# One written order for all steps of a windowed-attention and feed-forward kernel

## The chip, the core and the metric

The kernel runs on one core of a Trainium2 chip. The metric is the device time of one execution in microseconds (us); below it is the median of three runs. The engines are TensorE (PE in the rows; its weight loads PEld), VectorE (DVE), ScalarE (ACT), GpSimd (POOL) and SyncE (SP); ACTq and SPq are the instructions with which ScalarE and SyncE start transfers.

## What is computed

The reference, cut to its core (batch 8, 8 heads, 576 positions, head size 64; window 64; 4608 tokens of width 512; hidden width 2048):

```python
scores = scale * np.matmul(q, k.transpose(0, 1, 3, 2))
scores = np.where((rel >= 0) & (rel < window), scores, -1e9)
attn = np.exp(scores - scores.max(axis=-1, keepdims=True))
attn = attn / (attn.sum(axis=-1, keepdims=True) + 1e-09)
x = np.matmul(attn, v)                      # heads side by side: 4608 x 512
h = x @ w_in
out = np.maximum(0.01 * h, h) @ w_out
```

## The kernel before

**Work and stages.** The tokens form nine chunks of 512. Chunks 0 to 2 go through the two large products directly: `early_first` (tile h, line 1143) makes 128 hidden rows of one chunk in 12 matmuls, in two halves of 6; `leak` (line 1157), `high_of` (1160, ScalarE) and `low_of` (1163, VectorE) turn them into a high and a low part, and `early_second` (tile acc, line 1152) multiplies those with `w_out` in four groups of 3 matmuls, two turns later. The first half of chunk 0 and part of chunk 1 have the same work under other names (lines 679 and 715). Chunks 3 to 8 go in three pairs, each by seven products in place of eight: `product` (tile m, line 1344) for the first matrix, `seventh` (tile z, line 1410) for the second. Every operand is a high and a low float32r part, so a product is three matmuls.

**Attention** runs in 36 blocks of 128 tokens, between these matmuls. For block m: `mask_to` (ScalarE, line 876) writes the mask into two banks, `scores_of` (TensorE, 64 small matmuls, line 525) adds the scores, `copy_of` (ScalarE, 890) copies them out, `max_of` (GpSimd, 899) takes the maximum over partitions, `minus_of` (VectorE, 906) subtracts it, `exp_of` (ScalarE, 910), `add_of` (GpSimd, 902) sums, `values_of` (TensorE, 32 small matmuls, line 958) multiplies with v. `values_of` writes into one of the two banks that the h tiles use in turn, so it must wait until `low_of` of the last turn in that bank has read it. A stay of TensorE with one or more of these small steps between two large ones is called a visit here.

**Weights.** Until about 130 us, VectorE and ScalarE make float32 weights out of float64 words (`bits` 472, `sign` 476, `size` 480, `clamp` 484, `join` 489, `split` 492 with a store to `w_single`, `rest` 498). Then `prepare` makes sums of weights for the seven products: `whole_of` (VectorE, 1257) or a fetch (1253), four `join_of` (VectorE, 1260), `high` (ScalarE, 1263), `prep_low` (VectorE, 1266), and two stores `keep` issued by ScalarE (1270, 1273). `x_build` reads rows of x back (line 1091), makes sums of them by four `sub` (VectorE, 1098), and splits them by ScalarE (1117) and `x_low` (VectorE, 1120); the first `product` needs all of it.

**What sets the order.** Each engine runs its instructions in the order in which the program issues them. The first part (536 steps in the numbering below, to about 128 us) was issued from the hand-written string `ORDER`, before anything else. All later steps are entries of a list `plan`, made by `op`, each with its engine, a cost and the steps it comes after; `arranged` sorted them: `forward` runs the plan through a model of the engines, the transfers and a rule for GpSimd against VectorE (`port_rule`), `latest` gives each step a due time, and some rounds of both, 14 of them nudged at random, end in the order. Transfers issued by ScalarE and SyncE take turns through eight semaphores (`LANES = 8` in the model), so an issue waits until the eighth transfer before it has landed, and whatever stands behind it on the issuing engine waits too.

Of the kernel before, what the change touches and what calls it, by code (L numbers as in the profile page):

```python
# [26 lines left out]
P = 128  # L27
# [31 lines left out]
q0 X6 S0 k1 raw0 q1 E0 P0 E1 bits0 sign0 raw1 v0 q2 k2 P1 X3 Z0 Z1 S1 abs0 E2 N0 exp0 X1 N1 bits1 sign1 abs1 clamp0  # L59
join0 clamp1 V0 sm0 join1 exp1 V1 E3 S2 chi0 raw2 chi1 raw3 rec0 sm1 rec1 bits2 sign2 y1 y0 P2 P3 N2 raw4 E4 rest1  # L60
rest0 E5 exp2 N3 exp3 T0 v1 V2 V3 k3 q3 abs2 H0 S3 v2 v3 q4 k4 sm2 P4 sub4 P5 rec2 sm3 L0 y2 rec3 clamp2 y3 exp4 V4 E6
T1 join2 H1 sub5 sm4 bits3 rec4 L1 exp5 X4 V5 P6 raw5 chi2 sign3 abs3 E7 bits4 rest2 sub6 sm5 clamp3 rec5 y4 y5 sign4
P7 M0 lk0 exp6 gh0 M1 abs4 gl0 T2 W0 join3 sub7 bits5 clamp4 V6 lk1 H2 exp7 raw6 L2 gh1 join4 V7 S4 chi4 raw7 chi3 gl1
sm6 sign5 sm7 rest4 rec7 rec6 rest3 M2 E8 abs5 y7 y6 T3 bits6 sign6 W1 lk2 H3 L3 clamp5 P8 M3 gh2 gl2 join5 v4 k5 q5
E9 S5 v5 q6 k6 raw8 lk3 gh3 chi5 abs6 sub8 bits7 exp8 gl3 M4 lk4 rest5 sign7 clamp6 W2 V8 P9 abs7 sub9 join6 gh4 raw9
M5 bits8 gl4 E10 sm8 sign8 exp9 chi6 W3 P10 clamp7 rec8 y8 join7 rest6 lk5 abs8 clamp8 gh5 V9 M6 W4 gl5 join8 bits9
sub10 sm9 sign9 rec9 y9 raw10 E11 raw11 chi7 P11 chi8 lk6 exp10 T4 gh6 abs9 rest8 rest7 bits10 M7 V10 W5 gl6 sign10
clamp9 H4 abs10 sub11 join9 L4 bits11 sm10 rec10 clamp10 y10 join10 lk7 raw12 exp11 gh7 gl7 S6 V11 chi9 rest9 sign11
W6 chi10 raw13 abs11 E13 E12 P12 rest10 sm11 bits12 clamp11 join11 rec11 y11 chi11 raw14 sign12 abs12 bits13 sign13
clamp12 sub12 join12 M8 T5 v6 q7 v7 k7 W7 lk8 gh8 H5 exp12 abs13 chi12 raw15 gl8 P13 bits14 L5 V12 sign14 clamp13  # L70
rest11 sub13 sm12 join13 rest12 rec12 S7 y12 E14 raw16 abs14 exp13 clamp14 join14 bits15 P14 W8 V13 M9 sub14 sm13
sign15 chi14 E15 exp14 chi13 abs15 lk9 gh9 P15 rec13 y13 V14 T6 rest14 rest13 sub15 M10 sm14 clamp15 gl9 rec14 join15
y14 exp15 raw17 H6 chi15 V15 W9 bits16 sign16 L6 lk10 gh10 abs16 raw18 sm15 rec15 gl10 y15 T7 H7 rest15 W10 clamp16
bits17 join16 sign17 L7 abs17 clamp17 join17 bits18 raw19 chi16 ev0 chi17 ev1 raw20 rest16 sign18 abs18 rest17 M11
bits19 clamp18 M12 lk11 gh11 gl11 lk12 gh12 sign19 join18 M13 W11 M14 gl12 abs19 raw21 chi18 lk13 bits20 clamp19
join19 chi19 raw22 sign20 rest18 rest19 W12 M15 gh13 gl13 abs20 W13 bits21 clamp20 sign21 join20 bits22 abs21 lk14
sign22 clamp21 join21 raw23 chi20 M16 gh14 gl14 W14 rest20 raw24 abs22 clamp22 join22 chi21 raw25 bits23 rest21 sign23
bits24 lk15 chi22 gh15 gl15 sign24 abs23 abs24 clamp23 join23 bits25 chi23 raw26 lk16 M17 W15 clamp24 sign25 rest22
join24 M18 abs25 gh16 raw27 clamp25 gl16 rest23 join25 W16 chi24 rest24 bits26 sign26 lk17 chi25 rest25 raw28 abs26
gh17 bits27 clamp26 gl17 sign27 join26 abs27 clamp27 join27 chi26 lk18 chi27 gh18 bits28 sign28 rest26 gl18 k8 q8 v8  # L80
W17 q9
|
abs28 raw29 clamp28 join28 bits29 raw30 sign29 rest27 abs29 bits30 chi28 clamp29 sign30 rest28 abs30 join29 clamp30
raw31 chi29 bits31 sign31 rest29 abs31 join30 clamp31 chi30 join31 rest30 chi31 rest31
"""
FEW = 5
# [19 lines left out]
SLACK, AHEAD, ROUNDS = 0.0, 10.0, 4  # L106
NUDGES = (
    652231581, 285970256, 32845751, 566537775, 247891063, 817061414, 899342503, 908597559, 243672113, 194115331,
    115674943, 420121951, 340751465, 165549087,
)  # L110
LAGS = 1.0
ENTER, LEAVE, SIGNAL, SLOW = 0.12, 0.2, 0.07, 0.6
BOTH_SBUF = {
    "wide_low": 1.22, "combine": 1.22, "whole_of": 0.69, "prep_low": 1.22, "sub": 0.38, "join_of": 0.41, "x_low": None,
    "low_early": 0.68, "join": 0.69, "sign": 0.69, "rest": 0.69,
}
COSTS = {
    ("DVE", "inverse_of"): 0.19, ("DVE", "whole_inverse_of"): 3.35, ("DVE", "bits"): 0.42, ("DVE", "clamp"): 0.42,
    ("ACT", "guard_of"): 0.2, ("ACT", "wide_high"): 1.05, ("ACT", "high"): 1.05, ("ACT", "exp_of"): 0.63, ("ACT", "leaky"): 0.63,
    ("ACT", "high_early"): 0.63, ("ACT", "whole_guard_of"): 0.63, ("ACT", "split"): 0.63, ("ACT", "size"): 0.68,  # L120
    ("POOL", "max_of"): 1.87, ("POOL", "add_of"): 3.3, ("POOL", "fill"): 0.76, ("PE", "scores_of"): 0.97, ("PE", "values_of"): 0.97,
}
RATE, EACH, LANDING = 460.0, 100.0, 3.9
SIZES = dict(fill=1024, load_qk=512, load_v=512, fetch=512, fetch_w=512, keep=512, spread_of=128, rows_of=4, compact_of=2)
LONGER = dict(compact_of=0.5, spread_of=0.6, load_v=0.5, send=-2.7, reload_of=-1.5, fetch_w=-1.5, store=-1.2)


def measure(plan):
    for x in plan:
        f = x["fn"]  # L130
        name = x["name"] = getattr(f, "func", f).__name__
        e = x["engine"]
        x["both"] = e == "DVE" and (name in BOTH_SBUF or x["us"] > 1.0 and name in ("minus_of", "product_of"))
        x["reduce"] = name in ("max_of", "add_of")
        x["visit"] = name in ("scores_of", "values_of")
        x["dma"] = bool(x["land"])
        x["lane"] = x["dma"] and e != "POOL"
        if x["both"]:
            x["us"] = BOTH_SBUF.get(name, 0.67) or x["us"]
        elif (e, name) in COSTS:  # L140
            x["us"] = COSTS[e, name]
        elif e == "ACT" and x["land"]:
            x["us"] = 0.5
        elif e == "ACT" and x["us"] < 0.7 and name != "<lambda>":
            x["us"] = 0.59
        elif e == "DVE" and x["us"] < 1.0:
            x["us"] = 0.69
        x["bytes"] = EACH + x.get("size", SIZES.get(name, 256.0))
        x["more"] = LANDING + LONGER.get(name, 0.0)
        x["users"] = []  # L150
    for x in plan:
        for a in x["after"]:
            a["users"].append(x)


def gap(a, x, slack):
    if a["engine"] == x["engine"] and not a["dma"]:
        return 0.0
    return max(SIGNAL, x["lag"] * LAGS) + (slack if a["dma"] else 0.0)


def visiting(x, before):
    return x["us"] + (ENTER if x["visit"] and not before else LEAVE if before and not x["visit"] else 0.0)


def port_rule(x, t, port, held):
    end = t + x["us"]
    if x["both"]:
        held = end = (port[1] if port[0] <= t < port[1] else t) + x["us"]
    if x["reduce"]:  # L170
        end = max(t, held) + x["us"]
        port = end - x["us"], end - (0.9 if x["name"] == "max_of" else 1.12)
    return end, port, held


class Transfers:
    def __init__(self, rate=RATE):
        self.rate, self.queues, self.now, self.left = rate, {}, 0.0, {}

    def busy(self):  # L180
        return [q for q in self.queues.values() if q]

    def next(self):
        qs = self.busy()
        return min((self.now + self.left[q[0]["n"]] * len(qs) / self.rate for q in qs), default=None)

    def advance(self, t):
        qs = self.busy()
        for q in qs:
            self.left[q[0]["n"]] -= (t - self.now) * self.rate / len(qs)  # L190
        self.now = t

    def landed(self, t):
        self.advance(t)
        return [q.pop(0) for q in self.busy() if self.left[q[0]["n"]] <= 1e-6]

    def add(self, x):
        self.queues.setdefault(x["engine"], []).append(x)
        self.left[x["n"]] = x["bytes"]


def forward(plan, key, slack, due=None):
    free = dict.fromkeys(("PE", "DVE", "ACT", "POOL", "SP"), 0.0)
    waiting = {e: [] for e in free}
    missing = {x["n"]: len(x["after"]) for x in plan}
    for x in plan:
        if not x["after"]:
            waiting[x["engine"]].append((0.0, x))
# [3 lines left out]
    moving = Transfers()  # L212

    def begins(y):
        ready, x = y
        if x["lane"] and len(lanes) >= LANES:
            return max(ready, done.get(lanes[-LANES]["n"], math.inf))
        a = cleared(x)
# [20 lines left out]
    while True:  # L239
# [14 lines left out]
        if best is None:  # L254
            break
# [1427 lines left out]
```

## Time and profile before

| what | us |
|---|---|
| median of three runs | 842.6 (841.9 to 842.64) |
| the profiled execution, whole time | 840.71 |
| its span, first to last instruction | 838.9 |
| TensorE busy in it | 828.8 |

The time of an execution is its span and some 1.8 us around it. A row of a timeline or of the chain gives the start in us from the span's start, the duration, the engine, the line and the tiles (written <- read); xN is the number of instructions in the row, and the bracket is the engine's idle time before the row, with what ended it. Matmuls overlap: one of 128x512 is shown with 0.39 us, but the next begins 0.227 us after it.

### The profile page before, as it was taken

The numbers are of one execution on the slowest core, as the hardware profiler recorded it, in microseconds if no ns is written. First come the engines' busy times: TensorE is split into PE (matmuls) and PEld (weight loads), VectorE is DVE, ScalarE is ACT, GpSimd is POOL, SyncE is SP. The second block draws the span as 40 slices with busy tenths as digits, with TensorE's granted clock in tenths as the row PEclk, the third lists the DMA queues.
The fourth block names the chain that finished last, engine by engine and source line by source line (L and its number), as shares of the span: only waits on it lengthen the run. The fifth ranks groups of instructions, "written<-read, shape, count | busy, mean of one in ns | idle before, by whom it ended". The sixth has DMA issues, their size and how long they took to land.

```text
span 838.9 us, 16806 instructions
## 1 busy us (share of the span) xinstructions
PE 828.8 (99%) x6730; PEld 677.4 (81%) x6730; DVE 608.1 (72%) x869; ACT 426.6 (51%) x697; POOL 383.4 (46%) x216
## 2 busy tenths in 40 slices
PE   9999999999999999999999999999999999999998
PEld 5887888888887888788888888888888888888886
DVE  6999887546657888987558897654578965546953
ACT  4666556555645565655555553545444633324442
POOL 5423000977866864977786323877711111111110
PEclk9999999999999999999999999999999999999999
DMA  8874766789889879899999999899898986677784
GB/s 329 271 226 154 248 184 220 257 238 330 257 299 306 311 247 368 304 363 355 297 258 264 296 262 280 251 314 251 212 243 257 282 252 185 193 197 201 193 222 138
DMA packets 140782, 216.32 MB, mean 258 GB/s; under 512 B 15264, under 2 KB 72736, under 8 KB 140704
## 3 DMA queue, kind: packets, MB, share of 16 engines
q0 software_dynamic: 53568, 88.09, 39.0%
q10 hardware_dynamic: 46672, 68.92, 25.2%
q1 hardware_dynamic: 40464, 58.24, 21.2%
q8 instruction: 53, 0.87, 0.4%
q14 instruction: 25, 0.20, 0.1%
HBM read 162.04 MB, written 53.06 MB: 256 GB/s over the span
## 4 chain that ended last, share of the span: by engine, by line
PE 86%; DMA 7%; DVE 5%; SPq 1%; issue 1%; ACT 0%; ACTq 0%; DVEq 0%
PE m L1344 28%; PE z L1410 27%; PE h L1143 8%; PE acc L1152 8%; PE h L679 4%; PE acc L715 4%; PE s L525 3%; PE o L958 3%; DMA w_single<-w 1%; DMA more_v<-vL 1%; DMA w_second<-p 1%; DMA w_second<-pfew 1%; DMA w_first<-p 1%; DMA raw<-w_out 1%; PE o L615 1%
## 5 line engine op out<-in xcount | busy, mean ns | idle before, releaser
L1344 PE MATMUL m<-pfew,p 128*128 128x512 f32 x720 | 169.9, 391 | 0.0
L1344 PEld LDWEIGHTS m<-pfew,p 128*128 128x128 f32 x720 | 134.2, 188 | 28.7 <-DVE pfew L1120 0.2
L1410 PE MATMUL z<-gs,p 128*128 128x512 f32 x360 | 86.5, 389 | 0.0
L1152 PE MATMUL acc<-p,gs 128*128 128x512 f32 x324 | 79.3, 393 | 0.0
L1410 PEld LDWEIGHTS z<-gs,p 128*128 128x128 f32 x360 | 67.6, 188 | 14.0
L1410 PE MATMUL z<-pxa,p 128*128 128x512 f32 x324 | 78.0, 389 | 0.0
L1353 DVE TENSOR_TENSOR p<-m,pxa 128x512 f32<-128x512 f32 x60 | 41.4, 691 | 49.5 <-PE m L1344 48.9
L899 POOL PARTITION_ALL_REDUCE g<-late_f x20 | 37.8, 1940 | 82.4 <-ACT late_f L890 81.5
L1328 POOL DMA_DIRECT2D p<-w_first x42 | 31.8, 757 | 93.9 <-PE m L1344 55.8
L1353 DVE TENSOR_TENSOR pxa<-m,pxa 128x512 f32<-128x512 f32 x60 | 41.4, 689 | 43.5 <-PE m L1344 43.1
L1344 PE MATMUL m<-pxb,p 128*128 128x512 f32 x288 | 70.8, 392 | 1.3 <-DVE pxb L1120 1.2
L902 POOL PARTITION_ALL_REDUCE late_o<-late_f x20 | 66.4, 3339 | 12.3 <-DVE late_n L970 5.5
L1356 ACT ACTIVATE p<-p 128x512 f32<-128x512 f32 x60 | 37.5, 630 | 67.1 <-DVE p L1353 67.1
L1410 PEld LDWEIGHTS z<-pxa,p 128*128 128x128 f32 x324 | 60.7, 188 | 12.7
L1152 PEld LDWEIGHTS acc<-p,gs 128*128 128x128 f32 x324 | 60.0, 188 | 12.9
L902 POOL PARTITION_ALL_REDUCE late_o<-late_e x18 | 59.3, 3311 | 14.7 <-issue 9.4
L1344 PEld LDWEIGHTS m<-pxb,p 128*128 128x128 f32 x288 | 53.7, 188 | 13.2 <-DVE pxb L1120 1.6
L902 POOL PARTITION_ALL_REDUCE late_o<-e x18 | 60.3, 3373 | 5.6 <-DVE late_n L970 3.4
L1328 POOL DMA_DIRECT2D p<-w_sums x24 | 18.0, 750 | 95.0 <-PE z L1410 88.2
L1143 PE MATMUL h<-pxa,p 128*128 128x512 f32 x228 | 55.5, 391 | 0.0
L1410 PE MATMUL z<-third,p 128*128 128x512 f32 x216 | 51.9, 389 | 0.0
L1143 PEld LDWEIGHTS h<-pxa,p 128*128 128x128 f32 x228 | 42.6, 188 | 9.0
(192 smaller groups left out, 1676.8 us busy)
## 6 DMA issues: line engine op xcount, KB each, us to landing
p<-w_first POOLq DMA_DIRECT2D x42, 1024.0 KB, 6.7
p<-w_sums POOLq DMA_DIRECT2D x24, 1024.0 KB, 6.3
p<-w_second POOLq DMA_DIRECT2D x18, 1024.0 KB, 6.0
qk<-qk ACTq DMA_DIRECT2D x26, 512.0 KB, 6.3
raw<-w_out ACTq DMA_DIRECT2D x15, 512.0 KB, 4.1
raw<-w_in ACTq DMA_DIRECT2D x14, 512.0 KB, 3.8
more_v<-vL ACTq DMA_DIRECT2D x14, 512.0 KB, 7.2
late_r<-rows SPq DMA_DIRECT2D x54, 128.0 KB, 6.0
```

What stands on the lines that cost most here:

```text
L525: nc.tensor.matmul(ps[j][t, c : c + QB], k[i][s, p], q[s, w, p], start=not begun and (not more or (w, p) == (0, 0)), stop=not begun and no ...
L679: nc.tensor.matmul(ps, a[:, k, :], b[:, k, part], start=n == 0, stop=n == len(terms) - 1)
L715: nc.tensor.matmul(acc[c, i], a[:, ts], b, start=begin and n == 0, stop=end and n == 2)
L899: nc.gpsimd.partition_all_reduce(most_of(j), e_of(m)[:, j], P, ReduceOp.max)
L902: nc.gpsimd.partition_all_reduce(sum_of(j), e_of(m)[:, j], P, ReduceOp.add)
L1143: nc.tensor.matmul(ps, a[:, k, :], b[:, k], start=i == 0, stop=i == len(terms) - 1)
L1152: nc.tensor.matmul(acc[c, i], a[:, i * P : (i + 1) * P], b, start=begin and k == 0, stop=n in ends and k == 2)
L1328: nc.gpsimd.dma_start(to, of, max_dma_last_dim=2048)
L1344: nc.tensor.matmul(tiles[b], w[:, 256 * i + 128 * kt : 256 * i + 128 * kt + 128], x_part(OF_X[k], j, kt), start=begin and c == 0, stop=c = ...
L1353: nc.vector.tensor_tensor(to(), tiles[b], x(), ALU.add)
L1356: nc.scalar.activation(to(), to() if b is None else tiles[b], AF.Prelu, alpha=0.01)
L1410: nc.tensor.matmul(tiles[b + i], a, x, start=begin and f == 0 and c == 0, stop=f == half - 1 and c == 2, skip_group_check=not begin,)
```

## The change

The planner (`measure`, `forward`, `latest`, `nudged` and their tables) is removed. The steps of `ORDER` enter `plan` too, ahead of the others, and so do the four memory and copy steps that stood before them. Two steps are split so that a store is a step of its own: the store of `split` becomes `sw`, that of `evict` becomes `es`. `arranged` then issues `plan` in the order of a written list of 2880 numbers. The number of a step is its place in `plan`; matmuls, operands, tiles and transfers are the same. The edges "order of transfers" now link the first part's transfers as well, since they begin where `plan` begins. Cut:

```diff
-def forward(plan, key, slack, due=None):
...
+ON = {
+    "PE": "S Z N V T X M W", "POOL": "P", "SP": "q k v es", "ACT": "raw exp H abs chi sw lk gh ev kk eye far one",
+    "DVE": "E sub sm rec y L bits sign clamp join rest gl zero",
+}
+LIST = """
+5 0 6 9 1 14 10 2 7 16 3 4 11 13 8 17 15 22 19 25 31 12 27 18 28 24 72 32 23 46 20 33 26 30 34 40 37 35 36 42 38 49 44
+39 41 55 52 56 43 58 47 21 53 60 50 48 51 57 54 68 45 65 63 64 73 62 66 71 61 69 89 81 80 82 76 67 70 95 85 84 59 88
...
+1093 750 663 597 656 657 655 667 741 1094 733 651 668 669 751 732 752 735 765 769 670 1095 629 766 671 672 754 753 673
...
+1300 1331 955 1309 1332 958 1142 949 1149 961 1297 1151 1152 962 959 957 1333 967 1126 960 1301 1318 1336 963 1127
...
+1432 1839 1436 1422 1440 1193 1065 1206 1068 1207 1437 1194 1066 1434 1840 1841 1842 1843 1069 1435 1198 1844 1067
...
+"""
 def arranged(plan):
-    measure(plan)
...
+    order = [plan[int(n)] for n in LIST.split()]
     place = {x["n"]: i for i, x in enumerate(order)}
+    assert len(place) == len(plan) and all(place[a["n"]] < place[x["n"]] for x in plan for a in x["after"])
     return order
...
     def split(n):
         nc.scalar.copy(flat(parts(n)[0]), singles[n])
-        if n % 2 == 0:
-            nc.scalar.dma_start(w_single[n // 2], singles[n])
+
+    def put_single(n):
+        nc.scalar.dma_start(w_single[n // 2], singles[n])
...
-    for name in order.split():
-        step(name)()
...
+    for name in order.split():
+        kind, n = name.rstrip("0123456789"), int(name.lstrip(ascii_letters))
+        engine = next(e for e, kinds in ON.items() if kind in kinds.split())
...
+        op(engine, 0.5, step(name), land=5.0 if kind in MOVES.split() else 0.0)["step"] = name
...
-        o[kind] = op(engine, us, step(name), *(o.get(b) for b in before), *more, rank=0.3)
+        used = [weights_of.get(n - 2, {}).get(k) for k in ("rest", "sw")] if kind == "join" else []
+        o[kind] = op(engine, us, step(name), *(o.get(b) for b in before), *used, rank=0.3)
```

Numbers that the prediction speaks of:

| step | number |
|---|---|
| first q, raw weights 0, second q, first scores | 5, 9, 10, 7 |
| `bits` 0, the first two `shield` (VectorE, line 570) | 14, 11, 13 |
| `high_of`, `low_of` of turn 8; `keep` of one weight sum | 667, 668; 1094, 1095 |
| `scores_of` 11, `values_of` 9 | 751, 769 |
| `leak`, `high_of`, `low_of` of turn 19; load of v for block 16 | 947, 948, 949; 1289 |
| `low_of` 20; both halves of `early_first` 21; `scores_of` 17; `values_of` 15 | 960; 961, 962; 1318; 1336 |
| the two sums of block 16; those of block 21 (GpSimd) | 1301, 1303; 1436, 1438 |
| `whole_of`, three `join_of` of one weight sum | 1137; 1138, 1139, 1140 |
| the last four `sub`; the last three `x_low` | 1840 to 1843; 1845, 1847, 1849 |
| copy of a sum bank (`early_out`), third bank of chunk 2 | 1072 |

## Rows read from the trace of the kernel before

**Rows 1.** The page, busy us, share and instructions of two engines.

```profile
PE 828.8 (99%) x6730; PEld 677.4 (81%) x6730; DVE 608.1 (72%) x869; ACT 426.6 (51%) x697; POOL 383.4 (46%) x216
```

**Rows 2.** Windows: length; busy PE, PEld, DVE, ACT, POOL; clock; DMA share; GB/s.

```profile
0.00:12.00 12.00, 10.30 (x146) 6.58 (x146) 5.62 (x8) 4.04 (x7) 4.92 (x7) 1.00 0.84 310
12.00:25.00 13.00, 12.41 (x252) 8.88 (x252) 12.90 (x31) 8.61 (x17) 8.66 (x5) 1.00 0.97 332
25.00:88.00 63.00, 62.22 (x673) 50.05 (x672) 61.16 (x134) 41.24 (x77) 17.92 (x9) 1.00 0.66 206
...
170.00:270.00 100.00, 98.11 (x1091) 79.81 (x1083) 62.33 (x88) 53.67 (x99) 74.38 (x30) 1.00 0.89 292
...
340.00:347.00 7.00, 5.75 (x140) 4.49 (x138) 6.91 (x10) 3.50 (x8) 6.05 (x3) 1.00 0.93 332
347.00:834.00 487.00, 486.97 (x3286) 402.28 (x3286) 333.89 (x414) 228.09 (x339) 204.19 (x137) 1.00 0.90 253
834.00:839.00 5.00, 1.09 (x5) 0.56 (x3) 1.37 (x2) 0.00 (x0) 0.00 (x0) 1.00 0.28 105
```

**Rows 3.** The chain that ended last, in order of time: start, us, what.

```profile
200.65 2.72 PE h L1143 x12
...
204.45 2.94 PE acc L1152 x12
...
380.77 12.50 PE m L1344 x54
...
682.77 76.16 PE m L1344 x336
```

**Rows 4.** Waits of TensorE over the run: total us, times, longest.

```profile
PE o L958 <- DVE gs L1163: 1.6, 2, 1.2
...
PE m L1344 <- DVE pxb L1120: 1.2, 1, 1.2
```

**Rows 5.** Timeline of ScalarE, 180 to 184 us.

```profile
180.94 0.55 ACTq L1270 DMA_DIRECT2D w_sums<-pspare  x1
181.59 0.59 ACT L1160 CAST gs<-h 128x512 fp32r<-128x512 f32 x1 [3.02 <-DMA w_second<-pfew]
```

**Rows 6.** Timeline of ScalarE, 254 to 268 us.

```profile
258.61 0.57 ACTq L421 DMA_DIRECT2D v<-vL  x1
259.23 0.63 ACT L910 ACTIVATE late_e<-late_e 128x512 f32<-128x512 f32 x1 [4.38 <-DMA w_first<-p]
```

**Rows 7.** Timeline of VectorE, 254 to 268 us.

```profile
255.43 0.69 DVE L1257 TENSOR_TENSOR p<-pfew 128x512 f32<-128x512 f32 x1 [0.28 <-PE acc L1152]
...
260.97 1.83 DVE L1257 TENSOR_TENSOR p<-p 128x512 f32<-128x512 f32 x1
262.83 3.17 DVE L1260 TENSOR_TENSOR p<-p 128x256 f32<-128x256 f32 x3
265.93 0.68 DVE L1163 TENSOR_TENSOR gs<-h,gs 128x512 fp32r<-128x512 f32 x1
```

**Rows 8.** Timeline of GpSimd, 254 to 268 us.

```profile
260.01 3.23 POOL L902 PARTITION_ALL_REDUCE late_o<-late_e  x1 [4.39 <-issue]
263.49 3.23 POOL L902 PARTITION_ALL_REDUCE late_o<-late_e  x1 [0.24 <-ACT late_c L917]
```

**Rows 9.** Timeline of VectorE, 326 to 347 us.

```profile
340.67 3.83 DVE L1098 TENSOR_TENSOR p<-p 128x256 f32<-128x256 f32 x4
```

**Rows 10.** Timeline of GpSimd, 14 to 24 us.

```profile
16.88 1.78 POOL L580 PARTITION_ALL_REDUCE g<-e  x1 [1.46 <-ACT e L572]
19.91 2.00 POOL L580 PARTITION_ALL_REDUCE g<-e  x1 [1.25 <-DVE sm L622]
22.93 1.88 POOL L580 PARTITION_ALL_REDUCE g<-e  x1 [1.02 <-DVE sm L622]
```

**Rows 11.** Timeline of VectorE, 5 to 24 us.

```profile
6.49 1.29 DVE L570 SCALAR_TENSOR_TENSOR e<-s,p 128x512 f32<-128x512 f32 x2 [5.09 <-PE s L525]
7.69 0.90 DVE L472 TENSOR_SCALAR raw<-raw 128x512 uint32<-128x512 uint32 x1
```

More of the change, by code (lines that the diff above doesn't have):

```diff
@@ L103 @@
 REBIAS = 2.0 ** -112
[L106 to L153, printed above, removed]
@@ L156, in gap @@
[L156 to L173, printed above, removed]
@@ L176 @@
[L176 to L199, printed above, removed]
@@ L290, in latest @@
-def latest(order, links, slack):
-    _, users = links
-    late, pinned, t, before = {}, {}, 0.0, False
-    for x in order:
-        if x["engine"] == "PE":
-            if not x["visit"]:
-                pinned[x["n"]] = t
-            t += visiting(x, before)
-            before = x["visit"]
-    taken = {e: ([], []) for e in ("DVE", "ACT", "POOL", "SP")}
-    for x in sorted(order, key=lambda x: -x["begin"]):
-        land = x["end"] - x["begin"] - x["us"] if x["dma"] else 0.0
-        ends = [late[y["n"]] - gap(x, y, slack) - land for y in users[x["n"]]]
-        if x["n"] in pinned:
-            ends.append(pinned[x["n"]] + x["us"])
-        end = min(ends, default=t + 20.0)
-        if x["engine"] != "PE":
-            begins, stops = taken[x["engine"]]
-            i = bisect_left(begins, end)
-            while i and stops[i - 1] > end - x["us"] + 1e-9 and begins[i - 1] < end - 1e-9:
-                i -= 1
-                end = min(end, begins[i])
-            i = bisect_left(begins, end - x["us"])
-            begins.insert(i, end - x["us"])
-            stops.insert(i, end)
-        late[x["n"]] = end - x["us"]
-    return late
@@ L319, in sound @@
-def sound(order, links):
-    place = {x["n"]: i for i, x in enumerate(order)}
-    return all(place[a["n"]] < place[x["n"]] for x in order for a in links[0][x["n"]])
-def nudged(plan, late, seed):
-    r = Random(seed)
-    far, share = r.choice((0.5, 1.0, 2.0, 4.0)), r.choice((0.02, 0.1, 0.5, 1.0))
-    return {x["n"]: late[x["n"]] + (r.gauss(0.0, far) if r.random() < share else 0.0) for x in plan}
-def arranged(plan):
-    measure(plan)
-    order, links = forward(plan, {x["n"]: x["rank"] for x in plan}, SLACK)
-    for n in range(ROUNDS + 1):
-        late = latest(order, links, SLACK)
-        for seed in NUDGES if n == ROUNDS else ():
-            late = nudged(plan, late, seed)
-        order, links = forward(plan, late, SLACK, AHEAD and {x: t - AHEAD for x, t in late.items()})
-    assert sound(order, links)
+LIST = """
[115 rows of a table added]
@@ L849, in band_attention_ffn @@
             continue
+        if kind == "sw":
+            o["sw"] = bulk(step(name), o.get("join"), rank=0.3)
+            continue
         engine, us = ("ACT", ACTS) if kind in ("abs", "chi") else ("DVE", ONE)
@@ L1129, in band_attention_ffn @@
     ends = {n for n in range(len(walk)) if n + 1 == len(walk) or walk[n][0] != walk[n + 1][0]}
-    pair_at = [pairs_of_g[next(turns) % 2] for _ in walk]
+    pair_at = [pairs_of_g[(len(jobs) + n) % 2] for n in range(len(walk))]
     h_of, tiles, stage = {}, {}, {}
```

168 lines of the change are left out of this document (49 added, 119 removed), and 110 rows, old and new, of the table LIST.

## The prediction

> **What bounds the kernel now.** I read the page first: TensorE is busy for 828.8 of 838.9 us, VectorE for 72% and GpSimd for 46% [rows 1]. No engine but TensorE can give more than what TensorE waits, so the second view is the windows, to find where its 10.1 us of idle time lie [rows 2]. From 347 to 834 us it is idle for 0.03 us. 5 us at the end hold 1.1 us of matmuls, and the last sums and stores follow these; 1.7 us are missing in the first 12 us, before and around the first loads; 0.59 from 12 to 25 and 0.78 from 25 to 88, while VectorE is busy for 12.90 of 13 and 61.16 of 63 us. In the middle only two stretches have holes: 1.89 us between 170 and 270, and 1.25 between 340 and 347.
>
> Third, the chain shows the pace where nothing waits: 336 matmuls in 76.16 us, 0.2267 each [rows 3]. By this pace a group of 12 takes 2.72 us; after a visit it takes 2.94, and 54 between two visits take 12.50 in place of 12.24. So a visit costs 0.22 to 0.26 us beside its own small matmuls. A wait also empties the pipeline: a matmul is shown with 0.39 us and the next should start after 0.227, so each hole costs 0.16 more than its idle time.
>
> Fourth, what ends the holes. TensorE's waits name two `values_of` behind `low_of` (0.4 and 1.2 us) and one `product` behind `x_low` (1.2) [rows 4]; the 0.3 that is left of the 1.89 is an `early_first` at 261 us, also behind `low_of`. Why VectorE or ScalarE was late there is read in their timelines. At 180.94 ScalarE starts a store that had to wait for an older transfer to land; `high_of` 8 stands behind it and is 3.02 us late [rows 5]. At 258.61 it is the load of v, after 4.38 us, ahead of an `exp_of` and then of `high_of` 19 [rows 6]. From 260.97 VectorE is itself held: `whole_of` takes 1.83 us where the same step took 0.69 at 255.43, and three `join_of` take 3.17 [rows 7], while a sum on GpSimd runs from 260.01 and another from 263.49 [rows 8]; `low_of` 20 starts at 265.93 only. At 340.67 four `sub` take 3.83 us [rows 9] under the two sums of block 21, and the last `x_low` are late.
>
> **The change, part by part.** No matmul, operand or byte changes, so TensorE's work stays. I set the list against the order that the planner gives: on TensorE 130 of 664 places hold another step, on VectorE 742 of 869, on ScalarE 739 of 845, on GpSimd 84 of 212, on SyncE 253 of 290. Most steps move by a few places; on SyncE stores of weights go back by up to 70.
>
> *The four holes.* At 182 us the list has 667 (`high_of` 8) ahead of 1094 and 1095 (`keep`), so the store no longer stands before it. Its other conditions, the turn's `leak` and the matmuls that free its pair, are over by 180 us, and with 0.6 for ScalarE and 0.7 for VectorE the bank is free before 182.5. At 261 us 1289 (load of v) has left its place between 947 and 948 and stands ahead of 947. At 266 us 1137, 1138 and 1140 stand ahead of 949, so before 960 only 1139 and another weight's fourth `join_of` remain; and 1301, the sum that held them, comes later, since ScalarE's `exp_of` does. 962 now stands ahead of 1318, so 1318 and 1336 are one visit; `values_of` 15 itself comes no later by that. At 344 us 1840 to 1843 and 1845 come ahead of 1072, which waited for the last matmuls of chunk 2. What is late next is in each case the next step of TensorE, which has its operands. Worth, if all four go: idle 1.89 + 1.25 and 4 x 0.16, together 3.8 us. None going is 0.
>
> *Visits.* Counted in the list, there are 31 after the first part, in place of 34 (scores and values that stood apart now follow one another, as 1318 and 1336). 3 x 0.24 is 0.7 us. Some visits now run values before scores; no row has that order, so I bound it by nothing and by one more visit's price for each of the five, 1.2; nearest are the visits with scores first, which pay nothing between the two, so I take 0.
>
> *The start.* Three reductions of GpSimd wait 1.46, 1.25 and 1.02 us for their operands [rows 10]; the list brings forward the copies and small steps that feed them, and TensorE's 0.59 + 0.78 of idle time hang on them: up to 1.4 us. Against that, 14 (`bits` 0) moves ahead of 11 and 13, the first two `shield` steps. These ran at 6.49, right after the first scores; `bits` 0 ran at 7.69 without waiting [rows 11], so its weights had landed by then. The list asks for them one transfer of 256 KB earlier, 0.8 us at the 310 GB/s of [rows 2]: by 6.9 at the latest. With its 0.90 us the first `shield` starts between 6.49 and 7.8, and the first maximum, on which the first `take` and all later ones hang, up to 1.3 us later. So the start lies between 1.4 gained and 1.3 lost; I take 0.5 gained, because the later reductions have 3.7 us of slack to return and the early delay 1.3 at most.
>
> *The split stores and the chained transfers.* `sw` and `es` add no instruction. A `join` waits for the store two before it, as its buffer did already. That the first part's transfers are chained fixes an order that the engines' own order fixes within each queue; the cost is an issue held for the other queue, between 0 and the 4.38 us that one held issue took [rows 6], and I take 0 because both queues are long at work then.
>
> *New waits.* The old order was planned without holes too, and left four. Nearly every step of VectorE and ScalarE has new neighbours, so I put in 0.8 us, two holes of the smaller kind (0.3 to 0.4 idle, and 0.16 each, gives 0.5; with a margin); bounds are 0 and the 3.8 that the old order had.
>
> How long a new hold would be, the rows say: `whole_of` came free at 262.80 less its 0.69, 1.13 us before that sum ended at 263.24 [rows 7, 8]. [...]
>
> **Sum.** The profiled execution took 840.7 (span 838.9 and 1.8 around it). 840.7 - 3.8 - 0.7 - 0.5 + 0.8 = 836.5. The median of the runs is 1.9 above that execution, so 838.4. In one execution more or less 0.2%, 1.7 us, is about what a measurement can tell.
>
> **Rivals.**
> 1. *The holes move.* The eighth-transfer rule keeps the same number of transfers, and DMA is 0.89 to 0.92 busy there [rows 2]; what is taken from before one `high_of` is put before another step. If the two holes that a held issue made come back (0.56 and 0.44), VectorE's are half cured and the start loses 0.5, the gain is 3.8 - 1.0 - 1.4 + 0.7 - 0.5 - 0.8 = 0.8: 841.8. For it: four transfers stand in a row before 947. Against: each hole has its cause moved away by name. Chance 0.16.
> 2. *Slower: the load of v stands before `leak` 19.* 1289, two `keep` and a load of q and k are now issued before 947, which ran at 254.3. If they wait to 258.61 as the one did and then take 0.57 each [rows 6], `leak` starts at 260.9 and `high_of` at 261.5, where it ran right after the `exp_of` of 259.23, at 259.8; `early_first` 21 then stands 1.7 us longer than now. One such place is covered by the 5.0 us gained; from three on the kernel loses, and four give 4 x 1.7 - 5.0 + 0.8 = 2.6 lost, 845.2. Against: the load is also earlier in its queue, so the transfer it waits for is older. Chance 0.12.
> 3. *The start decides downwards.* If the 1.3 us at the first maximum are kept to the end, and the rest goes as forecast: 838.4 + 1.8 = 840.2, still faster. It is part of the forecast's case.
>
> **How the numbers follow.** Forecast (with 3) 0.72; rival 1 0.16; rival 2 0.12. The forecast's own range: no new holes and the start's best, 838.4 - 0.8 - 0.9 = 836.7, less the 1.9 by which one execution lay under the median: 834.8; upwards, all of 3.8 returned as new holes is rival 1. So 834.8 to 842.3, which takes in rival 1 and leaves out rival 2 and a little below. Faster by over 0.2% is the forecast's 0.72; the same 0.16; slower 0.12.
>
> **What would show it.** Right: TensorE idle from 170 to 270 under 0.5 us and from 340 to 347 under 0.4; no `values_of` behind `low_of` for over 0.3; `sub` four times in under 2 us; visits 31; first reduction at 7.3 to 8.5. Wrong: ScalarE rows with a transfer of 2 us or more standing ahead of `leak` or `high_of`, with idle TensorE beside them; or idle time growing between 347 and 606, where there is none to win and only new waits can appear.

## The result, and the profile after

**The changed kernel is slower: 847.37 us against 840.21, 9 runs each, ratio 1.0087 [1.0068, 1.0106].** The forecast was 838.4, with 842.3 as its upper end. (The 842.6 that stood for the kernel before was the median of three runs. It takes 839.5 to 840.3 in the medians of 9 to 35 runs that follow, so the sum started some 2.4 us too high and was further off than it looks.) The profiled execution of the changed kernel took 847.61, span 845.8, 6.9 more than the span before.

The page of the changed kernel shows TensorE busy for 1.8 us more than before (some matmuls ran at a lower granted clock, 0.61 from 9 to 12 us, below), and the other engines nearly as before [rows 1]:

```profile
PE 830.6 (98%) x6730; PEld 678.7 (80%) x6730; DVE 607.3 (72%) x869; ACT 419.2 (50%) x697; POOL 379.9 (45%) x216
```

Windows of the changed kernel, columns as in [rows 2]:

```profile
0.00:12.00 12.00, 7.98 (x79) 4.86 (x80) 6.03 (x9) 3.33 (x6) 3.89 (x6) 0.90 0.85 307
12.00:25.00 13.00, 12.93 (x292) 9.25 (x292) 9.90 (x25) 7.19 (x14) 8.09 (x4) 0.96 0.79 247
...
88.00:170.00 82.00, 81.28 (x476) 66.69 (x475) 59.23 (x104) 45.30 (x80) 13.99 (x7) 1.00 0.62 196
170.00:270.00 100.00, 100.00 (x1124) 82.23 (x1123) 66.10 (x94) 55.76 (x103) 76.75 (x30) 1.00 0.87 287
270.00:340.00 70.00, 69.08 (x645) 56.28 (x644) 60.64 (x81) 39.13 (x69) 46.49 (x21) 1.00 0.99 323
340.00:347.00 7.00, 5.50 (x112) 4.44 (x112) 5.92 (x12) 4.58 (x10) 4.69 (x3) 1.00 0.89 324
347.00:433.00 86.00, 84.36 (x799) 68.43 (x796) 58.11 (x82) 41.38 (x76) 66.01 (x36) 1.00 1.06 317
433.00:606.00 173.00, 172.27 (x1443) 141.76 (x1442) 123.50 (x158) 86.80 (x143) 101.78 (x61) 1.00 0.93 265
```

The 1.89 us of idle TensorE from 170 to 270 are gone. The 1.25 from 340 to 347 have become 1.50; 0.72 (88 to 170), 0.92 (270 to 340), 1.64 and 0.73 (347 to 606) are new, where the profile of the kernel before has nothing, or 0.03. From 88 us on that is 5.5 idle in place of 3.2. The start is worse by more: the 36 matmuls that ran at 87.82 begin at 90.86, from the same first matmul (1.45 and 1.44). TensorE's timeline, before and after, there and at the first product:

```profile
87.82 8.32 PE L679 MATMUL h<-pxb,pfew 128*128 128x512 f32 x36
...
343.74 0.50 PE L1344 MATMUL m<-pxb,p 128*128 128x512 f32 x1
```

```profile
90.86 8.32 PE L574 MATMUL h<-pxb,pfew 128*128 128x512 f32 x36
...
347.98 1.66 PE L1253 MATMUL m<-pxb,p 128*128 128x512 f32 x6
```

The changed kernel is 3.04 us behind at the 36 matmuls, 4.24 at the first product and 6.9 at the end, so it loses before, between and behind these rows. (One execution of each; how much executions differ is shown with the experiments.) TensorE's waits in the changed kernel name no `values_of` behind `low_of` any more, but these, which the kernel before did not have [rows 4]:

```profile
PE s L420 <- ACT s L783: 1.5, 2, 1.3
...
PE s L489 <- POOL g L475: 1.3, 1, 1.3
PE s L455 <- DVE e L465: 1.1, 1, 1.1
PE m L1253 <- DMA p<-w_first: 0.9, 2, 0.6
PE h L1050 <- ACT late_n L872: 0.9, 1, 0.9
PE h L1050 <- DVE gs L1070: 0.7, 1, 0.7
PE t L536 <- DVE y L529: 0.7, 1, 0.7
PE m L1253 <- DVE pxa L1262: 0.6, 1, 0.6
PE z L1319 <- DMA p<-w_sums: 0.6, 1, 0.6
```

Three of them, read in the engines' timelines. At 324 us `take_of`, which copies a block's values out of their bank (line 872), stands on ScalarE behind two fetches that wait for an older transfer:

```profile
321.82 1.40 ACTq L1162 DMA_DIRECT2D pspare<-w_single  x2
323.32 0.59 ACT L872 COPY late_n<-o 128x512 f32<-128x512 f32 x1 [3.68 <-DMA p<-x_rows]
```

At 344 us the four `sub` take 1.80 where they took 3.83 [rows 9], as forecast; but the `minus_of` of block 21 (line 813) now stands behind a copy that waits for TensorE (line 1082), `exp_of` behind that, and the next `mask_to` behind `exp_of` and two splits of x; TensorE comes to the scores of the next block and waits 1.3 us for that `mask_to`. The hole has another cause and the old size. VectorE:

```profile
341.05 0.69 DVE L1082 COPY p<-acc 128x512 f32<-128x512 f32 x1 [0.54 <-PE acc L1059]
341.66 0.68 DVE L813 TENSOR_TENSOR e<-s,g 128x512 f32<-128x512 f32 x1
342.26 1.80 DVE L1005 TENSOR_TENSOR p<-p 128x256 f32<-128x256 f32 x4
```

At the start the granted clock of TensorE falls. Windows of the changed kernel:

```profile
6.00:9.00 3.00, 0.91 (x21) 0.48 (x13) 2.61 (x4) 0.55 (x2) 1.49 (x1) 1.00 0.99 353
9.00:12.00 3.00, 2.65 (x8) 1.04 (x9) 2.93 (x5) 1.50 (x3) 2.21 (x2) 0.61 1.06 408
```

After 2.1 us without work in 6 to 9 it is 0.61 in 9 to 12 and 0.96 to 25 us; before it was 1.00 throughout. The filler matmuls (line 751 before: three right behind the first scores, at 6.36 us, and one at 10.39) now stand behind later steps. On SyncE the second k, loaded at 1.18 us before, now stands behind two loads of raw weights and the second q, at 2.58; its timelines, before and after (line 414 is now 308):

```profile
1.18 0.42 SPq L414 DMA_DIRECT2D qk<-qk  x1
```

```profile
1.18 0.42 SPq L351 DMA_DIRECT2D raw<-w_in  x1
1.64 0.43 SPq L304 DMA_DIRECT2D qk<-qk  x1
2.11 0.43 SPq L351 DMA_DIRECT2D raw<-w_out  x1
2.58 0.52 SPq L308 DMA_DIRECT2D qk<-qk  x1
```

### The profile page after: what moved, and what is told of

Same layout as the page of the kernel before. It is cut to its first block, busy times and chain, and to the rows that moved or that the text cites. A ratio compares the mean times of both kernels' runs of the same rounds, so it can differ in the third digit from the quotient of the medians.

```text
span 845.8 us, 16754 instructions
## 1 busy us (share of the span) xinstructions
PE 830.6 (98%) x6730; PEld 678.7 (80%) x6730; DVE 607.3 (72%) x869; ACT 419.2 (50%) x697; POOL 379.9 (45%) x216
## 4 chain that ended last, share of the span: by engine, by line
PE 50%; DMA 3%; POOL 2%; issue 2%; DVE 0%; ACT 0%; POOLq 0%; ACTq 0%
PE z L1319 25%; PE m L1253 22%; DMA p<-w_first 3%; PE o L865 1%; PE s L420 1%; POOL g L806 1%; DMA p<-w_sums 1%; POOL late_o L809 1%; POOL p L1237 0%; DVE qk L1333 0%; DVE late_e L813 0%; ACT late_e L817 0%; DVE p L1262 0%; ACT late_f L797 0%; POOLq L1237 0%
## 5 line engine op out<-in xcount | busy, mean ns | idle before, releaser
L1319 PEld LDWEIGHTS z<-third,p 128*128 128x128 f32 x216 | 40.5, 188 | 8.4
```

Of the source, the lines that this page charges most:

```text
L1319: nc.tensor.matmul(tiles[b + i], a, x, start=begin and f == 0 and c == 0, stop=f == half - 1 and c == 2, skip_group_check=not begin,)
```

## The experiments

Each kernel is the changed one with another list of the same 2880 numbers, so each computes all. Ratios are to the kernel before, run on the same chip beside it.

**Structure or order?** The order that the planner gave, written into the list:

```diff
-LIST = 5 0 6 9 1 14 10 2 7 16 3 4 11 ...
+LIST = 0 1 2 3 4 5 6 7 8 9 10 11 12 ...
```

> The changed kernel, with the old order written into its list: only the split stores, the chained transfers of the first part and the missing planner are left of the change. If the order alone costs the time, this is the kernel before within 0.2% (about 840), with holes of TensorE again near 182, 261, 266 and 344 us. If the split stores or the chained transfers cost it, this takes 844 to 847.

840.12, ratio 1.0005 [0.9988, 1.0022]. The split stores and the chained transfers cost nothing that can be measured; the loss is the order's.

**Which part of the order?** First the two parts, 536 steps and the rest:

```diff
-LIST = the changed list
+LIST = its first 536 steps, then the others in the order of before
```

> The first 536 steps in the new order, all later ones in the old. If the start is what costs (granted clock 0.61 between 9 and 12 us, 3 us behind at 88 us), this is 3 us above the kernel before: 843, and the four old holes are there. If the later steps cost all, it is 840.

```diff
-LIST = the changed list
+LIST = the first 536 steps in the order of before, then the others as changed
```

> The first 536 steps in the old order, all later ones in the new. If the start costs 3 us and the later steps the rest, this is 844 (847.4 less 3), still above the kernel before, with the clock at 1.00 throughout and new holes from 320 us on. If the start costs everything, because its delay carries the later holes with it, this is 837 to 839.

e2: 842.75, 1.0038 [1.0017, 1.0058]. e3: 843.18, 1.0034 [1.0016, 1.0051]. Each part loses about 3 us, and they add up to about what the whole loses. The rest was cut once more at the first product (344 us):

```diff
-LIST = the changed list
+LIST = 536 steps of before, the changed steps up to the first product, then before
```

> Old first part; the new order from there to the first product at 344 us, the old order after it. If the cures of the named holes work and little new comes with them, this is the best kernel so far: 2 to 3 us under the kernel before, 837 to 838. If new holes between 88 and 344 us (1.2 us at 321, 1.5 and 0.5 at 335 to 345 in the changed kernel) eat them, it is 840 to 841.

```diff
-LIST = the changed list
+LIST = the order of before up to the first product, then the changed one
```

> The old order to the first product at 344 us, the new order after it. If the late landings of weights in the products' ring and the held VectorE there (six new holes of 0.4 to 0.9 us after 348 us in the changed kernel) are what the later part costs, this is 3 to 4 us above the kernel before, 843 to 844. If they only follow from a bad state at 344 us, it is 840.

e5: 841.25, 1.0015 [1.0002, 1.0027]. e6: 842.22, 1.0022 [1.0007, 1.0037]. The stretch that the change was to mend loses as well.

TensorE's timelines say the same, and how much executions of one order differ. Each profile was cut at the start of the 36 matmuls, at the first product and at the end of the last matmul of the seven products (number of profiles in brackets):

| stretch | order of before, us | changed order, us | medians apart |
|---|---|---|---|
| up to the 36 matmuls | 87.41 to 91.85, median 88.1 (10) | 90.27 and 90.86 (2) | 2.5 |
| from there to the first product | 253.67 to 256.57, median 254.1 (10) | 255.13 to 257.11, median 256.2 (4) | 2.1 |
| from there to the last of the seven | 491.36 to 493.32, median 491.8 (8) | 493.58 to 495.84, median 494.4 (4) | 2.6 |

(Order of before: in the first row the kernel before, e1, e3, e5, e6, e8, e11, e13, e16, e17; in the second the kernel before, e1, e2, e6, e11 to e15, e18; in the third the kernel before, e1, e2, e12, e14 to e16, e18. Changed order: the changed kernel, with e2 in the first row, e3 to e5 in the second, e3, e4, e6 in the third.) The loss is spread over all three.

**The four cures alone**, then without the one at 344 us. They take away the causes that the prediction named, by fewer moves than the change and not to its places (the load of v, for one, goes behind `high_of` 19, where the change has it ahead of `leak` 19; what e16's text calls "as the change has them" is the cause and not the place):

```diff
 (order of before)
+663 669 667 1095 668   945 1136 948 1289 1301   1126 960 1140 962
+1070 1067 1840 1841 1842 1843   1847 1848 1435
```

> The old order throughout, but for eight moved steps that take away what made the four old holes: one store behind high_of 8, the load of v behind high_of 19, one join_of behind low_of 20, four sub ahead of early_out and one exp_of behind the last split of x. If the old holes are worth what the prediction counted (3.8 us), this is 836 to 837.5; if they come back elsewhere, 839 to 840.5.

```diff
 (order of before)
+663 669 667 1095 668   945 1136 948 1289 1301   1126 960 1140 962
```

> The order of before with the steps behind the holes at 182, 261 and 266 us moved as the change has them, and nothing at 344 us (e8_four_cures without its last moves; that gave 841.08, ratio 1.0011). If the three holes cost what they took on average (0.9 us): 838.8 to 839.3, TensorE busy 100.00 in 170 to 270. If the time is given back at 344 to 380 us whatever comes before: 839.7 to 840.5.

e8: 841.08, 1.0011 [0.9992, 1.0029]; e16: 841.37, 1.0010 [0.9991, 1.0029]. Both times lie a little above all that was expected of them, and both intervals rule out a gain of over 0.1%, 0.8 us. Windows of e8:

```profile
170.00:270.00 100.00, 100.00 (x1100) 81.85 (x1093) 64.57 (x91) 55.06 (x102) 75.17 (x31) 1.00 0.92 300
340.00:347.00 7.00, 5.93 (x69) 5.00 (x66) 5.85 (x9) 4.28 (x7) 5.22 (x2) 1.00 1.00 333
347.00:433.00 86.00, 83.39 (x766) 68.09 (x765) 56.46 (x86) 45.67 (x83) 67.41 (x37) 1.00 1.06 312
```

None idle in 170 to 270, but 1.07 from 340 to 347 and 2.61 from 347 to 433, together 3.68. The profile of the kernel before has 1.25 and 0.03 there; with the six others that have its order there (e1, e2, e12, e14, e15, e18) the two together are 1.28 to 2.28, so e8 has some 2 us more. TensorE's waits in e8 name what stands there, in place of the one `product` behind `x_low` (the third of these ends in 340 to 347):

```profile
PE m L1253 <- DMA p<-w_first: 1.5, 1, 1.5
...
PE m L1253 <- DVE pxa L1262: 1.1, 1, 1.1
PE o L865 <- ACT e L817: 1.1, 1, 1.1
```

In e16 two holes open near the ones that were cured, one at 263 us, where scores wait for a `mask_to`, and one behind 272; TensorE's waits in e16:

```profile
PE s L420 <- ACT s L783: 1.2, 1, 1.2
PE o L865 <- DVE gs L1070: 0.6, 1, 0.6
```

The first is made by the cure: the load of v no longer stands before `high_of` 19, but before `mask_to` 17, and has to wait as before (ScalarE in e16; line 315 is the load, 783 `mask_to`):

```profile
260.37 0.59 ACTq L315 DMA_DIRECT2D v<-vL  x1
261.00 1.05 ACT L1172 CAST p<-p 128x1024 fp32r<-128x1024 f32 x1 [5.25 <-DMA w_second<-p]
261.96 1.10 ACT L783 COPY s<-away 128x512 f32<-128x512 f32 x2
```

In e8, with the same order up to there, that load went out at 256.97 and no hole came.

And the 1.89 that was to be won had not been there to win in most executions. Ten profiles have the order of before in that stretch (before, e1, e2, e6, e11 to e15, e18); TensorE idles there for 1.89, 1.25, 0.37, 0.00, 2.60, 0.38, 0.01, 0.34, 0.02 and 0.58 us: 0.74 in the mean. In e6, for one, the first `exp_of` of block 16 started at 254.00 and not, as before, at 259.23 behind the held load of v.

**The start.** Fillers of the changed kernel put back:

```diff
-7 16 3 4 ... 58 47 21 53 ... 26 30 ... 93 78 29 97
+7 21 16 3 4 ... 58 47 53 ... 26 29 30 ... 93 78 97
```

> The changed kernel with two groups of filler matmuls (three and one) back at their old places, after the first scores and before the second take. If TensorE's clock is what the start costs, the clock stays at 1.00 from 9 to 25 us and 1.5 to 3 us come back: 844.5 to 846. If the start is late by VectorE's order (the first bits ahead of the first shield) and by late operands, the clock is whole and under 0.7 us come back.

844.9 in 7 runs, 1.0070 [1.0045, 1.0095]: the clock is 1.00, and the time lies between e3's and the changed kernel's, with intervals that overlap both; what the fillers give back in the whole kernel, 2.5 us by the medians, is not clear of the noise. So the two causes were tried one by one in the order of before (fillers away; the first N step, `21 22 27 23 24` in the list, ahead of the second Z step and scores; N is `take`, the matmul that needs GpSimd's maxima, line 489, and Z the matmul that adds a mask, line 455) and undone one by one in e2.

```diff
 (order of before)
-7 8 ... 20 21 22 ... 28 29 30
+7 8 ... 20 22 ... 58 21 59 ... 92 29 93
```

> The order of before; only the 3 filler matmuls between the first scores and the first values, and the 1 ahead of N1, are moved to where the changed order has them (behind N2, ahead of T1). If the fillers alone hold the clock: granted clock about 0.6 in 9 to 12 us, and 842 to 843 us. If the clock falls only together with the changed order of VectorE and GpSimd at the start, which makes TensorE wait: clock 1.00 and 839.5 to 840.5.

```diff
 (order of before)
-20 21 22 23 24 25 26 27 28
+20 21 22 27 23 24 25 26 28
```

> The order of before with that one step alone moved as the change has it: the first N step ahead of the second Z step and the second scores on TensorE. Fillers in their old place. Theory 1: TensorE loses about 1 us around 8 to 9 us, with the fillers the clock stays at 1.00; 840.2 to 841.2. If the step alone brings the clock down: 842 to 843 and a clock under 0.9 in 9 to 12.

```diff
 (e2_early_new)
-31 12 27 18 28 24 72 32 23 46
+31 12 18 24 72 32 23 27 28 46
```

> As e2_early_new (the changed order in the first 536 steps alone, 842.75 us), with one step of TensorE moved: the first N step, which waits for GpSimd's first reduction, goes back behind the second scores and the second Z step. The fillers stay where the change put them. Theory 1 (this one step leaves TensorE idle in 6 to 9 us, and the clock falls after it): TensorE busy 2 us or more of 6 to 9 (0.90 in e2), granted clock 1.00 in 9 to 12 (0.70 in e2), 840 to 841 us. Theory 2 (it takes the fillers, or bits0 ahead of the first shield on VectorE): busy under 1.5, clock under 0.9, 842 to 843.

```diff
 (e14_n0_back)
-7 16 3 4 ... 58 47 21 53 ... 93 78 29 97
+7 21 16 3 4 ... 58 47 53 ... 29 30 ... 93 78 97
```

> The changed order in the first 536 steps, the old one behind it (e2_early_new, 842.75 us), with both of TensorE's moves at the start undone: the fillers back in their place and the first N step behind the second scores and the second Z step. VectorE's, ScalarE's and GpSimd's order stay as changed. Theory 1 (the start loses through TensorE's idle stretch and the clock behind it, and these two moves make it): mean granted clock of the executions as before the change (0.999; e2 0.9975), 839.7 to 840.7 us. Theory 2 (bits0 ahead of the first shield on VectorE and the other moves cost by themselves): clock back, but 841.2 to 842.

| kernel | us | ratio | clock of 9 to 12 us in the profile | mean clock of all executions |
|---|---|---|---|---|
| e2 | 842.75 | 1.0038 [1.0017, 1.0058] | 0.70 | 0.9975 |
| e12, fillers away | 840.76 | 1.0007 [0.9994, 1.0019] | 1.00 | 0.9989 |
| e15, N step ahead | 841.0 | 1.0013 [0.9995, 1.0031] | 0.53 | 0.9990 |
| e14, N step back | 843.27 | 1.0033 [1.0016, 1.0049] | 0.69 | 0.9985 |
| e18, both back | 842.97 | 1.0033 [1.0018, 1.0049] | 1.00 | 0.9994 |

(The kernel before: 0.9992 over 30 executions; the changed one: 0.9963 over 9.) In e15 the N step leaves a hole of 1.5 us in which TensorE waits for GpSimd's first reduction, and the clock falls behind it though the fillers are in place. A hole there doesn't always bring that: in 6 to 9 us TensorE is busy for 1.68 us in e4 and 1.10 in e7 (below), and both have 1.00 from 9 to 12. Windows of e15:

```profile
6.00:9.00 3.00, 1.63 (x24) 0.81 (x16) 2.63 (x4) 0.56 (x2) 1.87 (x1) 1.00 1.02 405
9.00:12.00 3.00, 2.83 (x5) 1.50 (x5) 2.54 (x5) 0.68 (x1) 2.09 (x2) 0.53 1.06 409
```

But in e18 the clock is back in every window and the time is not. Theory 1 falls (and 842.97 is above what theory 2 gave too). Nor does the clock part e2's own executions: the three with a mean of 0.999 or more have a median of 842.49, the other nine 842.86. TensorE's waits in e18, to 88 us (beside the 1.4 at the first filler, which both have, these are 4.1 us; before there were 1.0):

```profile
PE t L536 <- DVE pxa L544: 1.2, 1, 1.2
PE s L420 <- DMA qk<-qk: 1.1, 2, 0.7
PE t L536 <- DVE y L529: 1.0, 1, 1.0
PE o L510 <- ACT e L494: 0.5, 1, 0.5
PE o L510 <- ACT e L496: 0.3, 1, 0.3
```

The second scores wait 0.7 us for a q and a k, of which SyncE now asks for the k 1.4 us later; the transposes wait for two steps of VectorE, the low part of x (line 544) and the scaling by the inverse sum (529). With the lower clock (0.61 from 9 to 12 us in the changed kernel, 1.00 in e18) the same start has little idle time (0.07 from 12 to 25 us in the changed kernel, 1.84 in e18), and the 36 matmuls begin at much the same time: 90.27 in e2, 89.99 in e18, 88.1 in the median with the order of before. So the start is bound by the steps that feed TensorE, and what the lower clock takes there was, as far as intervals of 0.16% tell, waiting time. Which move makes the 2 to 3 us was not tried: in e18 another step still stands at 20 places of TensorE, 189 of VectorE, 144 of ScalarE and 21 of SyncE (GpSimd's order at the start is the old one).

**The late part.** Five steps of the changed kernel that stood behind others that were not ready, moved ahead, with the fillers back:

```diff
 (e4_fillers_back)
+583 581 582 540   1401 1036 1398 1186 1187   1422 1440 1434 1193   1455 1890 1901 1472
```

> The changed kernel with the fillers back (as in the fourth run) and four more moves: low_of 0 ahead of the bits of weight 29, take_of 18 ahead of two fetches, minus_of of block 21 ahead of prep_low and early_out, one fill ahead of a maximum. If each new hole is made by the step named to stand ahead, 0.9 + 0.9 + 1.5 + 0.6, some 3 to 4 us come back: 841 to 842. If the holes move on to the next late step, under 1.5 come back: 843.5 to 845.

845.06 in 6 runs, 1.0066 [1.0041, 1.0090], against 1.0070 for e4: the holes at 138 and 324 us are gone from the profile, the time stays. A second theory was the weight loads of the seven products, which GpSimd issues between its reductions:

```diff
 (e6_new_from_344)
+1452 1858 1880 1453   1479 1913 1925 1480   1960 1956 1976 1547   2060 1591 2081 1622   2302 1730 2325 1734
```

> As e6_new_from_344 (842.22 us), with five weight loads of GpSimd's queue (the 4th, 8th, 13th, 22nd and 40th) moved ahead of the reductions that stand in front of them; in e6 these loads were issued 7.7 to 9.1 us before the first matmul that reads them, before the change 9.2 to 13.4 us. Theory 1 (loads behind reductions make the late part slow): TensorE's waits for p<-w_first and p<-w_sums, 1.5 us in e6, are gone, 840.5 to 841 us. Theory 2 (the late part loses through many small waits for VectorE and ScalarE, and the loads are one sign of it): 841.7 to 842.5, other waits take their place.

GpSimd's timeline, e6 and then e13. In e6 the load waits behind two sums of one row (6.45 us), in e13 behind one:

```profile
572.64 6.45 POOL L809 PARTITION_ALL_REDUCE late_o<-e  x2 [1.66 <-ACT e L817]
578.97 0.76 POOL L1237 DMA_DIRECT2D p<-w_first  x1
```

```profile
573.07 3.23 POOL L809 PARTITION_ALL_REDUCE late_o<-e  x1 [1.34 <-issue]
576.18 0.76 POOL L1237 DMA_DIRECT2D p<-w_first  x1
```

From 347 to 606 us TensorE idles for 2.53 in e6 and 0.27 in e13; e13's windows:

```profile
347.00:433.00 86.00, 85.92 (x775) 70.48 (x774) 59.47 (x84) 43.30 (x81) 64.74 (x36) 0.99 1.04 308
433.00:606.00 173.00, 172.81 (x1478) 141.93 (x1477) 121.75 (x157) 84.83 (x138) 104.72 (x62) 1.00 0.94 264
```

840.65, 1.0009 [0.9992, 1.0027]: the late loads go with the idle time behind 347 us. That they are the loss there is not shown: the intervals of e6 and e13 overlap, and in the profiles the stretch from the first product to the last of the seven takes 495.84 in e6, 494.61 in e13 (with a hole of 2.0 us and a clock of 0.91 at 340 to 347) and at most 493.32 with the order of before. Then both mends on the whole late part:

```diff
 (e3_early_old)
+583 581 582 540   1401 1036 1398 1186 1187   (and the five loads of e13)
```

> The first 536 steps as before, the rest as changed (e3_early_old, 843.18 us), with the five weight loads of e13_fills_ahead ahead of the reductions, and the two steps behind the new holes at 138 and 324 us moved as in e7_mended (the low parts of the first shift ahead of the weights' bit steps; the layer norm's last step ahead of two fetch issues). If the late part's loss is these named holes: 843.2 less 1.6 (the loads, from e13) less up to 1.6 (the two holes) = 840 to 841.6. If holes that are closed come back elsewhere (as between 344 and 380 us in e8 and e16): 842 to 843.

842.22, 1.0034 [1.0012, 1.0057], as e3 without them. No wait for a weight load is left in its profile, yet it idles 1.73 us from 347 to 433 and 0.92 to 606, now for a load of q and k (1.0) and for VectorE (0.8 and 0.6). The mends are no cure outside e13. (What e17's text calls the layer norm's last step is `take_of` 18; the kernel has no layer norm.)

**Can one queue be judged alone?** The order of the other four engines as before with GpSimd's as changed, and the reverse (e10 with the fillers back, e11 behind 344 us only):

```diff
 (order of before)
+GpSimd's 212 steps in the changed order
```

> Steps in the order of before on TensorE, VectorE, ScalarE and SyncE; GpSimd alone runs its 212 steps in the order of the changed kernel. Theory 1 (the part of the loss that does not lie at the start comes from GpSimd's queue: weight loads issued behind reductions, as the one of 457.6 to 468.4 us after a late first product): slower than before, 842 to 843 us, TensorE waits for p<-w_first and p<-w_sums between 380 and 600 us. Theory 2 (it comes from VectorE's and ScalarE's queues, where steps stand behind others that are not ready): as before, 839.5 to 840.5.

```diff
 (e4_fillers_back)
+GpSimd's 212 steps in the order of before
```

> The changed kernel with the two groups of filler matmuls back at the start (as in e4_fillers_back, 844.9 us) and with GpSimd's steps in the order of before; the other four engines as changed. Theory 1 (GpSimd's queue): 841 to 842, no TensorE wait for a weight load above 0.3 us between 380 and 600. Theory 2 (VectorE's and ScalarE's queues): 844.5 to 845.5, as e4.

```diff
 (e6_new_from_344)
+GpSimd's 212 steps in the order of before
```

> The order of before up to the first product, the changed order from there (as e6_new_from_344, 842.22 us), but GpSimd in the order of before. Theory 1: 840 to 840.5; the 0.6, 1.1 and 1.0 us that TensorE lost at 395, 460 and 580 us are gone. Theory 2: 842 to 842.5 and the losses stay.

874.06 (1.0395 [1.0361, 1.0430]), 898.49 (1.0710 [1.0679, 1.0742]) and 891.03 (1.0600 [1.0577, 1.0623]). Both theories are far off: another step at 84 places of one queue (61 in e11) costs 34 to 54 us when the others don't go with it. These three say nothing of where the 7 us come from.

## Why the prediction was wrong

Its sum was 840.7 - 3.8 - 0.7 - 0.5 + 0.8, and three of the terms were off by some 3 us each, all to one side. (To this the 1.9 by which three runs lay above the profiled execution was added, though 840.7 was already above the medians of all later runs. The range's upper end, 842.3, is no sum of its terms either: 838.4 with new waits at their bound, 3.8 in place of 0.8, is 841.4. Neither changes the outcome.)

**The four holes, 3.8.** Each cause was read rightly, and what was said of the steps came true: no idle TensorE from 170 to 270, four `sub` in 1.80 us, no `values_of` behind `low_of`. What failed is the size. It was taken from one execution in which the three early holes cost 1.89, while the same order has 0.74 in the mean of ten: they hung on when a transfer landed (a store at 182, the load of v at 261 and, by the sum that came late, at 266), which differs between executions (0.00 to 2.60 us of idle TensorE in the ten). The 0.16 a hole beside its idle time is borne out: from the 36 matmuls to the first product e15 takes 253.67 with 0.02 idle, the kernel before 255.92 with 1.89 in three holes, 0.13 more for each. The hole at 344 us does recur (1.2 from 340 to 347 in the mean of the ten), but it kept its size with a new cause, against the sentence that the next step of TensorE "has its operands": the scores that it came to next did not have their `mask_to`. The sum should have had some 1.1 here, 0.74 and three times 0.13; e8 and e16 show no gain at all.

**The start, 0.5 gained (range 1.4 gained to 1.3 lost).** e2 measured 3.2 lost by its ratio. `bits` 0 ahead of the shields, the one price that was worked out, costs 0.2: the first shield started at 6.73 in place of 6.49, the first reduction at 7.51 in place of 7.28, inside the 7.3 to 8.5 that was given. What failed is the choice of what to price. The moves of TensorE, SyncE and ScalarE there were not costed, and "the later reductions have 3.7 us of slack to return" took a gain from waits that the new order replaced with others: TensorE's are 4.1 us to 88 us in e18, 1.0 before. Of the moves that were tried, the N step and the fillers cost nothing clear of the noise alone (e15, e12), and undoing both (e18) did not bring the time back; the second k behind two loads of raw weights is 0.7 of the 4.1. Which of the other moves costs the rest stays open.

**New waits, 0.8.** The rest of the order loses 2.9 (e3), a net that already holds what the cures give, so the new waits are worth 3 to 4: near the bound of 3.8 that the old order gave, not near two small holes. e16 shows one way: a step moved out of the way of one wait stood before the next one. Of the nine kinds of wait that are new in the profile, six lie behind 88 us, of 0.6 to 1.3 us each. The sign named in the prediction, idle time growing between 347 and 606, came: 2.4 us. The 0.03 that it was to grow from was a low one, though: the seven profiles with that order have 0.03 to 1.48, 0.7 in the mean, all of it up to 433; behind 433 they have 0.00, and the changed kernel 0.73. In e13, where five loads stand further ahead, the 2.4 is 0.3; in e17, with the same loads, it is back.

**Visits, 0.7.** The count is right, 31 in place of 34; the worth is too small to see beside the rest. **Structure, 0:** right, within the 0.17% of e1's interval.

**The rivals.** Rival 2 was right that the kernel got slower, but not in why: the load of v ahead of `leak` 19 left no wait in 170 to 270. Rival 1, holes that move, was the mechanism, for 344 us and behind it; but it was given 0.16 and only as a smaller gain, since it let no hole grow beyond those that had been there. The chance of a loss, 0.12, was far too low for an edit that puts another step at 742 of 869 places on VectorE of a kernel in which nearly nothing waited.

**VectorE held by GpSimd**, the prediction's cause of the holes at 266 and 344 us, was not reduced in all: counted over each trace, VectorE's `TENSOR_TENSOR` instructions that took over 0.2 us more than the median of their line and shape are 51 before and 51 after, each of them beside a reduction on GpSimd, and what they took beyond it sums to 50.6 and 53.8 us. The rows of before had shown only the holds that reached TensorE.

## What to carry to other kernels

In a kernel that already keeps its main engine busy for 99% of the span, a new order can win little more than the idle time that recurs from execution to execution: take several profiles before pricing a hole, and set against it every step that leaves a place where it waited for nothing. A step that catches the eye at a hole need not be what the hole costs: fillers and clock, the first suspects at the start here, gave nothing back that could be measured. Undo it alone before calling it the cause. The queues' orders are one schedule: try an edit of it as a whole or a few steps at a time, never one engine's order against the others' old one.

## What was not expected of the hardware

**The clock.** A hole of 1.5 us at 8 us, with the fillers in place (e15), was followed by a granted clock of 0.53 in 9 to 12 us; e7, with more idle time there, and e18, with hardly a hole before 9 us (2.84 busy of 3), stayed at 1.00. So one profile doesn't tell what a hole does to it, and the mean clock of an execution ranges from 0.995 to 1.000 over twelve executions of one kernel (e14). In the kernel before it goes with the time: of the 134 executions beside the experiments, the 98 with a mean of 0.999 or more have a median of 839.3, the 36 below it 842.1. Whether the clock makes the difference or the holes that come ahead of it (the next paragraph has some) is not shown. In the changed kernel's profile the first 9 us had 1.00, and the fall came behind them; in e18 against e2 the clock of 9 to 12 us came back (1.00 in place of 0.70) and the time did not (842.97 and 842.75).

**A wait without a releaser.** In some executions (e1, e9, e13 and e17 among the profiles, all with the order of before at the start) TensorE stands for 1.5 to 3.1 us before one group of scores at 22 to 24 us, and the profile finds nothing that it waited for. In e1:

```profile
24.09 0.27 PE L420 MATMUL s<-p 64*64 64x64 f32 x1 [3.14 <-issue]
```

That execution took 844.75 where the median of the kernel is 840.12, and the kernel before spreads from 837.9 to 845.1 too. What the wait is was not settled. With such a spread, differences under 0.2% of this kernel are unclear even with 12 runs.
